# Block 0 of a fused attention and GLU kernel loaded as pairs of tokens, with attention by token parity and the gate by tanh

## The chip, the cores and the metric

The kernel runs on one core of one Trainium2 chip. The metric is the device time of one execution, in microseconds (us), as the median of several executions. The kernel before repeats within 0.4%.

Engines: PE is TensorE's matmuls, PEld its weight loads, DVE VectorE, ACT ScalarE, POOL GpSimd, SP SyncE. POOL, SP and ACT also issue the DMA loads and stores.

## The reference

Linear attention with decay over four batches, eight heads, 768 tokens and head size 64, then a gated feed-forward layer over the 3072 tokens (512 to 1536 to 512):

```python
# attention, per batch and head, token i, j <= i:
out[i] = sum_j (q[i] . k[j]) * lam[h] ** (i - j) * v[j]      # computed in blocks, with a state
x      = out.transpose(0, 2, 1, 3).reshape(B * S, H * D)
# feed-forward
gate = 1.0 / (1.0 + np.exp(-(x @ w_gate)))
val  = x @ w_val
return (gate * val @ w_out).astype(np.float32)
```

## The kernel before

Tokens are taken in six blocks of 128 per batch. Block 0's attention comes first, alone; then, for each block, twelve slices of gate and value products, four output products, and the next block's attention woven in between. The opening is what the argument touches: the loads of q, k and v of block 0, one token per partition, so 64 numbers, 256 bytes, per piece.

```python
def load(n, what, b0=0, b1=B):
    ...
        if b0 < nat:
            nc.gpsimd.dma_start(out=T_[c, n][:, b0:nat],
                in_=src[b0:nat, :, sl, :].rearrange("b h s d -> s (b h) d"))
...
load_hw("k", 0, nc.sync)          # k of batch 0, fp32, issued by SyncE
nc.scalar.dma_start(out=lam_bc, in_=lam.partition_broadcast(128))
load_hw("k", 1, nc.scalar)        # k of batch 1, issued by ScalarE
load(0, "q", 0, 2)                # the rest by GpSimd, cast to bf16 on the way
... identity, iotas, selects ...
load(0, "k", 2, 4)
load(0, "q", 2, 3); load(0, "q", 3, 4)
load(0, "v", 0, 2); load(0, "v", 2, 3); load(0, "v", 3, 4)
for ft in range(4):
    load_gv(ft, ft + 1)           # weights of the first slices: WG, WV
```

While these loads are on their way, PE is kept going with products of zeros (`zeros(9)` first). The gate of a slice and the loads of a later block:

```python
nc.scalar.activation(sg, gp, AF.Sigmoid)                 # sg in bf16
nc.vector.tensor_mul(HT[n, ft], sg, vp)
...
def next_loads(n):                # called for n = 2 in the slices of block 1
    xbar(n)                       # DMA transposes of q and k
    gate(n)                       # POOL waits here for the transposes
    load(n, "v")
    if n + 1 < NSTEP:
        load(n + 1, "qk")
```

## Time and profile before

| | before |
|---|---|
| time | 224.5 us median (224.48 to 224.63) |
| span in the profile | 222.8 us |
| first gate product starts | 15.23 us |
| gate products of blocks 1, 2, 3 start | 52.65, 86.69, 120.67 us |
| last output product ends | 219.86 us |

The rows below the first two are read from the timeline of PE, by the names of the tiles (gp for gate). From block to block PE needs 34 us.

### The profile page before, as it was taken

The page shows a single profiled execution, that of the slowest core. Times are in us where ns is not written, and L with a number is a line of the kernel's source. Part 1 is how long each engine was busy: PE and PEld are TensorE (multiplying, and loading weights), DVE is VectorE, ACT ScalarE, POOL GpSimd, SP SyncE. Part 2 cuts the span into 40 slices and gives each one's busy share as a digit, 9 for nine tenths or more (in the row PEclk, how much of TensorE's full clock was granted, in tenths as well). Part 3 has the DMA queues.
Part 4 walks back from the last instruction along what each step waited for, and adds up shares of the span by engine and source line. Part 5 has one row for each costly group of instructions (what it writes and reads, how often), then busy time and mean ns, then how long its engine had stood idle before and what let it go on. Part 6 is the DMA issues. An engine that isn't in the chain of part 4 may idle for free.

```text
span 222.8 us, 5208 instructions
## 1 busy us (share of the span) xinstructions
PE 215.8 (97%) x2187; PEld 105.7 (47%) x2187; DVE 104.4 (47%) x196; ACT 106.4 (48%) x232; POOL 64.0 (29%) x83
## 2 busy tenths in 40 slices
PE   6799999999999999999999999999999999999994
PEld 1454444557444544444544444544444544444443
DVE  4885652539777600785700686700676400333301
ACT  5877434594384523385433376342366342333221
POOL 7999855660094006700940030000000000000000
PEclk9999999999999999999999999999999999999999
DMA  6999999999989997999899995012100012100022
GB/s 108 152 169 182 195 203 178 175 156 156 176 55 158 235 153 214 179 162 176 56 157 231 223 63 36 3 50 94 47 3 0 3 50 94 47 0 0 4 94 96
DMA packets 106008, 25.25 MB, mean 113 GB/s; under 512 B 97152, under 2 KB 103552, under 8 KB 105984
## 3 DMA queue, kind: packets, MB, share of 16 engines
q0 software_dynamic: 82944, 13.90, 81.1%
q1 hardware_dynamic: 21712, 10.69, 20.4%
q10 hardware_dynamic: 1328, 0.33, 0.7%
q8 instruction: 17, 0.28, 0.5%
q14 instruction: 7, 0.06, 0.1%
HBM read 28.32 MB, written 6.29 MB: 155 GB/s over the span
## 4 chain that ended last, share of the span: by engine, by line
PE 91%; POOL 4%; DMA 3%; issue 1%; ACT 0%; POOLq 0%
PE po L523 28%; PE vp L488 28%; PE gp L488 28%; DMA WV<-in_moe_w_val_dram 3%; POOL vb L96 1%; PE sp L387 1%; PE cp L447 1%; PE op L411 1%; PE op L425 1%; POOL qb L96 1%; POOL WG L107 1%; POOL kb L96 1%; PE cp L363 1%; PE sp L310 0%; PE op L341 0%
## 5 line engine op out<-in xcount | busy, mean ns | idle before, releaser
L488 PE MATMUL gp<-XT,WG 128*128 128x512 bf16 (+1 forms) x296 | 74.2, 374 | 0.3 <-ACT XT L588 0.3
L488 PE MATMUL vp<-XT,WV 128*128 128x512 bf16 (+1 forms) x292 | 74.1, 376 | 0.1
L500 ACT ACTIVATE sg<-gp 128x512 bf16<-128x512 f32 x72 | 43.0, 597 | 62.9 <-PE gp L488 62.9
L505 DVE TENSOR_TENSOR ht<-sg,vp 128x512 bf16<-128x512 bf16 x48 | 33.0, 687 | 79.9 <-PE vp L488 76.9
L523 PE MATMUL po<-WO,ht 128*128 128x512 bf16 (+2 forms) x300 | 63.9, 371 | 0.0
L488 PEld LDWEIGHTS <-WV 128*128 128x128 bf16 x292 | 28.5, 98 | 33.7 <-DMA WV<-in_moe_w_val_dram 0.6
L523 PEld LDWEIGHTS <-ht 128*128 128x128 bf16 x300 | 28.3, 98 | 31.9
L488 PEld LDWEIGHTS <-WG 128*128 128x128 bf16 x296 | 28.2, 98 | 31.9 <-DMA WG<-in_moe_w_gate_dram 0.7
L527 ACT COPY ob<-po 128x512 f32<-128x512 f32 (+1 forms) x24 | 13.7, 572 | 38.8 <-PE po L523 38.8
L129 ACT ACTIVATE kd<-kb,kds 128x128 bf16<-128x128 bf16 (+1 forms) x88 | 28.9, 401 | 0.0
L503 DVE TENSOR_TENSOR ht<-sg,vp 128x512 bf16<-128x512 bf16 x24 | 16.5, 687 | 13.5 <-PE vp L488 13.3
L616 POOL COPY gates<-qt 128x1 bf16<-128x1 bf16 x4 | 0.8, 188 | 49.0 <-DMA qt<-qb 49.0
L96 POOL DMA_DIRECT2D vb<-in_v_dram x9 | 11.9, 1334 | 2.8 <-issue 1.7
L318 DVE TENSOR_TENSOR MT<-sp,mask 128x512 bf16<-128x512 f32 x16 | 9.9, 684 | 3.0 <-PE sp L310 3.0
L437 ACT CAST XT<-op 128x512 bf16<-128x512 f32 x16 | 8.2, 599 | 5.0 <-PE op L425 5.0
L397 DVE TENSOR_TENSOR MT<-sp,mask 128x512 bf16<-128x512 f32 x16 | 10.3, 683 | 0.0
L102 POOL DMA_DIRECT2D qb<-in_q_dram x10 | 8.8, 892 | 3.4 <-DMA WO<-in_moe_w_out_dram 3.2
L96 POOL DMA_DIRECT2D qb<-in_q_dram x8 | 8.9, 1115 | 1.8 <-POOLq L757 0.8
L102 POOL DMA_DIRECT2D kb<-in_k_dram x10 | 8.9, 913 | 1.1 <-DMA WG<-in_moe_w_gate_dram 0.6
L537 PE MATMUL zps<-st 128*128 128x512 bf16 x18 | 6.1, 471 | 1.5 <-DVE st L161 1.5
L96 POOL DMA_DIRECT2D kb<-in_k_dram x6 | 7.0, 1174 | 0.5 <-DMA WG<-in_moe_w_gate_dram 0.5
L110 POOL DMA_DIRECT2D WV<-in_moe_w_val_dram x9 | 7.1, 807 | 0.2 <-issue 0.2
(81 smaller groups left out, 114.3 us busy)
## 6 DMA issues: line engine op xcount, KB each, us to landing
out_dram<-ob SPq DMA_DIRECT2D x19, 256.0 KB, 2.3
vb<-in_v_dram POOLq DMA_DIRECT2D x4, 512.0 KB, 7.4
qb<-in_q_dram POOLq DMA_DIRECT2D x6, 256.0 KB, 7.7
kb<-in_k_dram POOLq DMA_DIRECT2D x6, 256.0 KB, 9.2
qb<-in_q_dram POOLq DMA_DIRECT2D x12, 128.0 KB, 7.5
WO<-in_moe_w_out_dram POOLq DMA_DIRECT2D x4, 384.0 KB, 12.3
kb<-in_k_dram POOLq DMA_DIRECT2D x10, 128.0 KB, 9.4
WG<-in_moe_w_gate_dram POOLq DMA_DIRECT2D x4, 256.0 KB, 7.0
```

What stands on the lines that cost most here:

```text
L96: nc.gpsimd.dma_start(out=T_[c, n][:, b0:nat], in_=src[b0:nat, :, sl, :].rearrange("b h s d -> s (b h) d"))
L102: nc.gpsimd.dma_start(out=T_[c, n][:, m:b1, u::2, :], in_=src[m:b1, 1 - u::2, sl, :].rearrange("b h s d -> s (b h) d"))
L129: nc.scalar.mul(KD[n][:, at, i, :], T_["k", n][:, at, i, :], kds[:, min(n // FIRST_XBAR, 1), h:h + 1])
L318: nc.vector.tensor_tensor(out=MT[n, b][:, u], in0=SP[n, b][u], in1=mask0[:, 1 - u if swapped(n, b) else u], op=ALU.mult)
L397: nc.vector.tensor_tensor(out=MT[n, bp][:, u], in0=SP[n, bp][u], in1=mask[:, u ^ bp].unsqueeze(1).to_broadcast([128, 2, HP, L]), op=ALU.mult)
L437: nc.scalar.copy(XT[n][:, c, :, bp * C:(bp + 1) * C], OP[n, c, bp].rearrange("p h j i -> p h (j i)"))
L488: nc.tensor.matmul(ps[:, part], lhsT=W[:, mt, fs], rhs=XT[n][:, part, mt], start=(part is not second and mt == 0), stop=(part is not first ...
L500: nc.scalar.activation(sg, gp.rearrange("p a b -> p (a b)"), AF.Sigmoid)
L503: mul = nc.vector.tensor_mul(HT[n, ft], sg, vp.rearrange("p a b -> p (a b)"))
L505: mul = nc.vector.tensor_mul(HT[n, ft].rearrange("p (b c i) -> p c b i", b=B, c=2), sg.rearrange("p (c b i) -> p c b i", c=2, b=B), vp.rea ...
L523: nc.tensor.matmul(po[:, :c1 - c0], lhsT=HT[n, ft][:, tt * 128:(tt + 1) * 128], rhs=WO[:, ft, c0:c1], start=(ft == 0), stop=(ft == NFT - 1))
L527: (eng.copy if eng is nc.scalar else eng.tensor_copy)(o, po[:, :c1 - c0])
```

## The change

Its intent: block 0's loads read two neighbouring tokens per partition, so 512 bytes per piece instead of 256, since DMA looks like what holds the opening. Partition p holds tokens 2p and 2p+1; partitions 0 to 63 hold the even heads, 64 to 127 the odd ones. The attention of block 0 is then done in 64x64 tiles by token parity. Most tables move behind the first slices. The gate becomes (tanh(x/2) + 1) / 2, with tanh in the same table set as exp.

```diff
+    def pairs(src, b0, b1):
+        return src[b0:b1, :, 0:C, :].rearrange("b (r g) (p e) d -> g p b r (e d)", g=2, e=2)
+    def load0(c, b0, b1):
+        ...
+        for g in range(2):                       # two halves of 64 partitions
+            nc.gpsimd.dma_start(out=T_[c, 0][rows_of(g), b0:b1]...,
+                                in_=src[g].rearrange("p b r x -> p (b r) x"))
     def load_hw(c, b, eng):
-        eng.dma_start(out=H32[c, b], in_=src[b, :, 0:C, :].rearrange("h s d -> s h d"))
+        for g in range(2):
+            eng.dma_start(out=H32[c, b][rows_of(g)]..., in_=pairs(src, b, b + 1)[g, :, 0])
...
+    nc.scalar.preload_act_table_set("exp_and_others")      # early
-    nc.scalar.preload_act_table_set("sigmoid_and_others")  # was in the masks
...
-                nc.scalar.activation(sg, gp..., AF.Sigmoid)
+                nc.scalar.activation(sg, gp..., AF.Tanh, scale=0.5)      # sg now fp32
-            mul = nc.vector.tensor_mul(HT[n, ft], sg, vp...)
+        mul = gate_value(HT[n, ft], sg, vp...)  # scalar_tensor_tensor: (sg + 1) * vp
-            (eng.copy ...)(o, po[:, :c1 - c0])
+            (eng.mul ...)(o, po[:, :c1 - c0], 0.5)
...
-    zeros(9)
+    zeros(6)
... t_0, s_0, a_0, c_0: block 0's transposes, scores, outputs and state in 64x64 tiles
... store_0: block 0's rows stored by parity, 14 stores instead of 8
```

The two halves per load follow from the layout: heads go with the half, so a single load for both halves has a source with one stride more.

## The prediction

> **What bounds the kernel now.** I read the page first, then the chain that ended last, then the waits and the timeline of the first 18 us. Columns of the page's first part: busy us, share, instructions.
>
> ```profile
> span 222.8 us, 5208 instructions
> PE 215.8 (97%) x2187; PEld 105.7 (47%) x2187; DVE 104.4 (47%) x196; ACT 106.4 (48%) x232; POOL 64.0 (29%) x83
> ```
>
> PE is full: 97% with no other engine over half. The chain in order of time (start, us, what) shows where PE is not yet the limit:
>
> ```profile
> 7.14 2.90 POOL vb L96 x3
> 10.04 0.75 POOL WG L107
> 10.79 0.74 POOL WV L110
> 11.53 0.67 POOL WG L107
> 12.21 5.81 DMA WV<-in_moe_w_val_dram
> 18.02 0.05 issue
> 18.07 1.04 PE vp L488 x4
> 19.10 0.86 PE gp L488 x4
> ```
>
> Up to 18.07 the chain runs over POOL, which issues the loads, and one weight transfer; from there it is matmuls, 0.86 us for each group of four, to the end. So **a change can only win by starting the first gate product (15.23 us) earlier, by removing holes just behind it, or by removing PE work.** The waits between 14 and 30 us (total us, times, longest) name the holes:
>
> ```profile
> PEld L488 <- DMA WG<-in_moe_w_gate_dram: 0.7, 2, 0.5
> PEld L488 <- DMA WV<-in_moe_w_val_dram: 0.6, 1, 0.6
> PEld L585 <- DMA vb<-in_v_dram: 0.4, 1, 0.4
> PE gp L488 <- ACT XT L588: 0.3, 1, 0.3
> ```
>
> Everything just before the first product waits for loads: the last v, the first WG, and the second WV (PE should have gone on at 17.85 and starts at 18.07: 0.2 us lost). The same loads seen from DMA, in the stretch 8 to 13 us:
>
> ```profile
> DMA packets 6137, 0.78 MB, mean 155 GB/s; under 512 B 6137, under 2 KB 6137, under 8 KB 6137
> q0 software_dynamic: 6137, 0.78, 243.5%
> ```
>
> That is 1227 pieces per us, 128 bytes written each (256 read). The stretch 14 to 17 us, which carries weights (512 bytes read, 256 written), has 707 pieces per us and 180 GB/s. In both DMA is busy in every slice, and the issues land 5 to 6 us after they are made: **a backlog, so DMA and not POOL sets the landings today**, though the chain, which follows issue by issue, prints POOL.
>
> [...] The gate product takes 687 ns for 512 elements, while 1024 elements of bf16 from SBUF take 685 ns (the scaling of QS)[...], and the gate in fp32 rather than bf16 should cost nothing there.
>
> **The change part by part.**
>
> *Pieces.* After the change a batch (256 KB read) is 512 pieces instead of 1024. At the rates above it takes 0.72 us of DMA (512/707) instead of 0.83 (1024/1227). The 10 batches of q, k and v that POOL loads cost 7.2 us instead of 8.3. DMA gains 1.1 us, and something on the two k batches that SP and ACT load.
>
> *Issues.* A half of the partitions per issue makes 14 issues out of 7. POOL's start-to-start times before: 0.735 us for a weight slice of 512 pieces (10.00, 10.74, 11.47, 12.21), 0.93 for 1024 (two in 1.87), 1.15 for 2048. So about 0.60 plus 0.27 per 1024 pieces, a fit of mine. Then 512 pieces cost 0.74, 256 cost 0.67. New: 6 halves of two batches, 4.4; 8 halves of one batch, 5.4; sum 9.8 us. Old: 1.28 + 1.15 + 1.87 + 2.87 = 7.2. Plus 2.6. POOL's own operations ahead of the first weight (identity, three iotas, two selects: 8.75 less 7.2, some 1.6 us) shrink to identity and one iota, some 0.6. Net: the first WG is issued at 1.25 + 9.8 + 0.6 = 11.65 us, not at 10.00.
>
> *Landings.* POOL now feeds a single batch in 1.34 us (two halves) that DMA moves in 0.72, so the backlog disappears and a landing is its issue plus an unloaded lag. The v load at 128.69, alone on the queue, gives that lag: issue ends at 130.38, the first packets come after 131.0, the last about 135.1, it lands at 135.8. So 0.8 ahead of the transfer and 0.7 behind it, plus up to 0.3 of ramp. First WG: 11.65 + 0.74 + 0.8 + 0.72 + 0.7, ramp included about 14.9 (before: 10.00 + 5.2 = 15.2). Last v: issued by 11.65, lands about 13.7 (before 14.4). Second WV: 11.65 + 3 x 0.74, lands about 17.1, needed at gp start + 2.6 = 17.5: the 0.2 us hole goes. Gates 4 and 5: issued after eight slices (5.9) and the iotas moved here (0.8), at 18.35, plus 0.74 + 0.8 + 1.44 + 0.7, 22.0; needed 7 groups and the split one later, gp start + 6.9 = 21.8. A hole of 0 to 0.4 us can open there.
>
> *The attention of block 0.* DVE: eight mask products of 0.68 each. Before they ran 8.85 to 11.33 and 11.89 to 14.37, the second stretch held by the q loads. Now q lands earlier (2: about 9, before 10.3), so both stretches run nearly as one, from about 8.5 to 13.8; two evictions behind them give about 14.8. ACT gains a second table load (1.28 us, at about 4.6, before exp) and loses the one at 12.32, and 4 of 5 early exps of 0.32 each move behind the products. DVE gets four wide exponents instead of eight narrow ones of 344 ns. PE's tiled products double in number at half the size: chunks of other blocks do 64 products of 64x64 in 0.74 us, so 16 take about 0.3 with latency, as before. The swap product (0.39) was in a hole anyway. None sets the end alone, but all meet near 14.8 to 15.0.
>
> *Steady state.* tanh for sigmoid, fp32 gate, factor 0.5 in the eviction: same element counts; 0.60 on ACT and 0.69 (perhaps 0.75) on DVE against 1.73 us of PE per slice. Eight query tables come behind slices 6 and 7, 1.28 us each plus 0.60 is 1.88, over 1.73 by 0.15, absorbed by a spare PSUM buffer. The state update K=64 has 64 products in about 0.7 us against 0.63 before. Stores go from 8 to 14 on SP, 0.66 us each: the transposes behind come 4 us later; the earlier (q) lands at about 88 and is used at 92.74. Hidden.
>
> *Sum.* First product 15.23 to about 14.95: minus 0.3. Hole at 17.85: minus 0.2. Hole at gates 4: plus 0.1 on average. 224.5 - 0.3 - 0.2 + 0.1 = **224.1 us**.
>
> **Rivals.** (1) *DMA alone counts*: if issues in halves are cheaper than my fit, or DMA was the only limit, v and WG land 1 us or more earlier. DVE then bounds: 5.5 us of products and two evictions. 223.0 to 223.4. For it: saturated DMA today. Against: the 0.735 us issue hardly falls with pieces. (2) *POOL takes DMA's place and is worse*: if a half costs 0.85 instead of 0.7, the first WG lands 2 us later than reckoned, and so does gates 4: 225.5 to 226. For it: slice issues did drift from 0.79 to 0.87 while the queue was full. Against: it will not be full. (3) *Row tiles collide*: two 64-row tiles write one PSUM bank in the output and state products. [...] The old chunk code gives each row tile its own bank, so this trace cannot tell. Serial, 16 products take about 0.9 instead of 0.4: plus 0.5 on the last batch, plus 2 on the state update; 225 to 226.5. (4) *Nothing*: all cancels, 224.4.
>
> **Range and chances.** PE after 15.23 is untouched, so 2% (4.5 us) faster would need the first product before 11 us, when not even the masks are done. Slower by 4.5 needs rivals 2 and 3 together and a new hole. The range spans from rival 1 to mild 2 or 3: **222.9 to 225.4**. Faster 0.02, within 2% 0.95, slower 0.03.
>
> **What would show it.** Right: POOL's L-lines of block 0 with 14 halves of about 0.7 us each; first WG issued near 11.65 and landing within 3.5 us of its issue, not 5.2; DMA below full between 6 and 13 us; first gate product at 14.6 to 15.2; no wait for the second WV; PE busy unchanged to 1 us. Wrong: landings still 5 us behind issues (the backlog stayed), a gate product before 14.2, a wait for gates 4 over 0.5 us, output products in the start over 0.8 us per batch, or PE waiting for DVE or ACT after 20 us.

The 1.28 us of a table load are those of the two in the trace before, at 1.68 and 12.32 us.

## More of the kernel before

The prediction shows the page, the chain and the waits. Here is the opening's timeline before, cut to the key and query path (kb, tk: keys; qb, tq: queries; zps: products of zeros; MT: the first of the products with the masks). Columns: start, duration, engine (SPq is SyncE issuing), line, operation, out<-in, count; in brackets the engine's idle time before it and what ended that.

```profile
0.74 0.45 SPq L152 DMA_DIRECT2D h<-in_k_dram  x1
1.53 3.49 PE L537 MATMUL zps<-st 128*128 128x512 bf16 x9 [1.53 <-DVE st L161]
5.37 0.41 DVE L293 CAST kb<-h 128x512 bf16<-128x512 f32 x1
5.84 0.40 PE L267 MATMUL tk<-ident,kb 128*128 128x128 bf16 x4 [0.82 <-DVE kb L293]
...
7.45 0.62 PE L267 MATMUL tq<-ident,qb 128*128 128x128 bf16 x8 [0.56 <-DMA qb<-in_q_dram]
...
8.85 2.48 DVE L318 TENSOR_TENSOR MT<-sp,mask 128x512 bf16<-128x512 f32 x4 [0.54 <-PE sp L310]
...
15.23 1.05 PE L488 MATMUL gp<-XT,WG 128*128 128x256 bf16 x8 [0.30 <-ACT XT L588]
```

The first queries (tq at 7.45) are waited for; from there everything to the first gate product follows in 7.78 us. PE is idle for only 0.82 us after the first zeros.

The load stream in the stretch 11 to 18 us, before:

```profile
DMA packets 6341, 1.19 MB, mean 170 GB/s; under 512 B 6340, under 2 KB 6340, under 8 KB 6340
```

## The result, and the profile after

The kernel after gives correct results and takes **228.11 us** (227.43 to 228.66, four runs) against 224.56 us (224.48 to 224.69, four runs) in the same rounds: ratio 1.0156, 95% interval 1.0127 to 1.0185. A ratio is the mean time of one kernel's runs over that of the other's of the same rounds, so it is not quite the ratio of the medians quoted. Executions over 1.5% slower than the fastest of the same kernel are left out of the means. That is still within the 2% band, but 3.5 us slower, outside the range of 222.9 to 225.4. It also spreads over 1.2 us, the kernel before over 0.2.

| | before | after |
|---|---|---|
| span in the profile | 222.8 | 225.7 |
| first gate product | 15.23 | 17.48 |
| gate products of block 1 | 52.65 | 54.74 |
| of block 2 | 86.69 | 89.51 |
| of block 3 | 120.67 | 123.49 |
| last output product ends | 219.86 | 222.68 |

So 2.25 us are lost before the first gate product, 0.16 come back in block 0, 0.73 are lost in block 1, and nothing from block 2 on. (The profiled execution, 227.43 us, was the fastest of the four.)

The page's first part after:

```profile
span 225.7 us, 5469 instructions
PE 216.6 (96%) x2302; PEld 107.3 (48%) x2311; DVE 104.4 (46%) x192; ACT 107.8 (48%) x236; POOL 65.7 (29%) x89
```

PE's busy time has grown by 0.8 us only: the rest is idle time of PE. The opening's timeline after, the same path:

```profile
0.74 1.45 SPq L167 DMA_DIRECT2D h<-in_k_dram  x2
1.25 1.50 POOL L114 DMA_DIRECT2D qb<-in_q_dram  x2 [0.81 <-POOLq L812]
1.53 2.74 PE L608 MATMUL zps<-st 128*128 128x512 bf16 x6 [1.53 <-DVE st L177]
6.80 0.70 DVE L363 CAST kb<-h 128x512 bf16<-128x512 f32 x1 [2.58 <-DMA h<-in_k_dram]
7.56 0.64 PE L290 MATMUL tk<-ident,kb 128*64 128x128 bf16 x8 [3.28 <-DVE kb L363]
8.13 1.46 PE L608 MATMUL zps<-st 128*128 128x512 bf16 x3
...
8.46 3.22 POOL L114 DMA_DIRECT2D vb<-in_v_dram  x5 [0.52 <-DMA qb<-in_q_dram]
...
9.52 1.06 PE L290 MATMUL tq<-ident,qb 128*64 128x128 bf16 x16
...
11.69 5.05 DVE L307 TENSOR_TENSOR MT<-sp,mask 128x512 bf16<-128x512 f32 x8 [1.06 <-PE sp L300]
...
17.48 1.12 PE L558 MATMUL gp<-XT,WG 128*128 128x256 bf16 x8
```

Three things differ. SyncE takes 1.45 us to issue the keys of batch 0 in two halves (before 0.45 in one), and the cast waits for them until 6.80 (before it could run at 5.37). PE is idle for 3.28 us. And then PE is slow: three products of zeros take 1.46 us, where three took 0.81 before. They start 0.43 us apart here, 0.22 in the steady state (0.86 us for each group of four). I call the first half rate and the second full rate; a warm PE is one that runs at full rate. The kernel before starts at half rate too: its first zeros are 0.43 us apart up to 4.43 us, after 2.9 us of zeros (in a_warm below it takes 5.4). The six zeros of the kernel after end before that, at 4.27, and none of them is faster. So this trace does not show PE at full rate before the gap at all; whether it fell in the gap or had never risen stays open. The page's row of the granted clock does not help in these two kernels; it reads 9 (90% or more) in every slice of both, over the slow first zeros as well. So that the missing zeros and the idle gap made PE slow is a reading, which a_warm below tests.

The issues on POOL: the load of q starts at 1.25, as before, and takes 1.50 us in two halves (before 1.28 in one). Between two halves of v, POOL stands 0.52 us until the queries have landed, at 8.17 us; why it has to wait for them, the runs leave open. The first WG is issued at 11.65 us. The load stream in the stretch 8 to 13 us, and in 11 to 18 us:

```profile
DMA packets 3183, 0.78 MB, mean 155 GB/s; under 512 B 3183, under 2 KB 3183, under 8 KB 3183
q0 software_dynamic: 3183, 0.78, 160.8%
...
DMA packets 3561, 0.89 MB, mean 127 GB/s; under 512 B 3560, under 2 KB 3560, under 8 KB 3560
```

In the first stretch half the pieces carry the same bytes. In the second, DMA moves 0.89 MB where it moved 1.19 before. The row of its busy share still reads 9 in most slices, but the time of its packets falls from 204.2% of the engines' span to 136.6%. I read this as DMA not being fed; a_best2 below supports it.

The waits between 14 and 30 us hold no load at all any more; the first of PE's are of 0.2 to 0.4 us behind work of ACT and its own issue. PE starts so late that all weights are there. But the chain of work that ended last has changed. In order of time, before 72 us:

```profile
2.06 6.11 DMA qb<-in_q_dram
...
20.38 6.25 DMA WG<-in_moe_w_gate_dram
...
30.88 13.49 DMA WO<-in_moe_w_out_dram
...
45.52 9.94 DMA qb<-in_q_dram
...
58.86 4.92 DMA kt<-kb
...
64.19 7.14 DMA vb<-in_v_dram
71.33 0.04 issue
71.37 0.73 PE cp L514 x60
```

Before, the chain went over to PE at 18.07. After, it runs along the loads until 71.33, where the values of block 2 land, and the state products that need them (cp) start at once. In the kernel before these values land at about 69.1 (issued at 62.01, 7.1 us to landing), and cp starts at 69.12. Counted from the start of the last group ahead of it that is 1.01 us; the same change from 128x128 to 64x64 products takes 0.95 to 0.96 where nothing is waited for (62.16 to 63.12, 74.11 to 75.06). So cp waited 0.05 us at most for them. In b_tanh, which takes the same time, PE waits 0.22 us for them, at 69.33. **So the kernel before stood at two limits at once**, PE and the load stream, and its chain printed PE's side of a near tie. In the trace after, both came late together.

A last 0.3 us: the first products of the attention of block 2 have a hole of 0.32 us at 78.24 which waits for nothing in the profile. Of the other kernels' profiles only a_kwide's has it (0.82 us at 79.59). I did not find its cause.

### The profile page after: what moved, and what is told of

Same layout as the page of the kernel before. It is cut to its first block, busy times and chain, and to the rows that moved or that the text cites. A ratio compares the mean times of both kernels' runs of the same rounds, so it can differ in the third digit from the quotient of the medians.

```text
span 225.7 us, 5469 instructions
## 1 busy us (share of the span) xinstructions
PE 216.6 (96%) x2302; PEld 107.3 (48%) x2311; DVE 104.4 (46%) x192; ACT 107.8 (48%) x236; POOL 65.7 (29%) x89
## 4 chain that ended last, share of the span: by engine, by line
PE 67%; DMA 21%; POOL 7%; issue 2%; SPq 1%; ACT 0%; POOLq 0%
PE po L594 23%; PE gp L558 20%; PE vp L558 20%; DMA qb<-in_q_dram 7%; DMA WO<-in_moe_w_out_dram 6%; DMA vb<-in_v_dram 3%; DMA WG<-in_moe_w_gate_dram 3%; DMA kt<-kb 2%; POOL WV L121 2%; POOL WG L118 2%; SPq L368 1%; POOL vb L114 1%; PE op L478 1%; PE cp L514 1%; PE op L492 1%
## 5 line engine op out<-in xcount | busy, mean ns | idle before, releaser
L548 DVE SCALAR_TENSOR_TENSOR ht<-sg,vp 128x512 bf16<-128x512 f32 x72 | 49.4, 686 | 92.9 <-PE vp L558 90.0
L570 ACT ACTIVATE sg<-gp 128x512 f32<-128x512 f32 x72 | 43.0, 597 | 59.5 <-PE gp L558 59.5
L598 ACT ACTIVATE ob<-po 128x512 f32<-128x512 f32 (+1 forms) x24 | 14.0, 583 | 38.7 <-PE po L594 38.7
L143 ACT ACTIVATE kd<-kb,kds 128x128 bf16<-128x128 bf16 x80 | 25.2, 390 | 0.0
L464 DVE TENSOR_TENSOR MT<-sp,mask 128x512 bf16<-128x512 f32 x16 | 10.3, 682 | 0.0
L96 POOL DMA_DIRECT2D vb<-in_v_dram x6 | 9.0, 1501 | 3.3 <-issue 1.6
L102 POOL DMA_DIRECT2D qb<-in_q_dram x10 | 8.8, 893 | 2.9 <-DMA WO<-in_moe_w_out_dram 2.9
L102 POOL DMA_DIRECT2D kb<-in_k_dram x10 | 8.9, 913 | 1.2 <-DMA WG<-in_moe_w_gate_dram 0.6
L539 DVE SCALAR_TENSOR_TENSOR st<-st,pow_l,cp 128x128 bf16<-128x128 bf16 x24 | 6.7, 341 | 0.0
L118 POOL DMA_DIRECT2D WG<-in_moe_w_gate_dram x8 | 6.6, 825 | 0.0
L96 POOL DMA_DIRECT2D kb<-in_k_dram x5 | 5.9, 1180 | 1.5 <-issue 1.2
L96 POOL DMA_DIRECT2D qb<-in_q_dram x5 | 5.8, 1153 | 0.4 <-DMA WO<-in_moe_w_out_dram 0.4
```

Source lines behind the costliest of these rows:

```text
L96: nc.gpsimd.dma_start(out=T_[c, n][:, b0:nat], in_=src[b0:nat, :, sl, :].rearrange("b h s d -> s (b h) d"))
L102: nc.gpsimd.dma_start(out=T_[c, n][:, m:b1, u::2, :], in_=src[m:b1, 1 - u::2, sl, :].rearrange("b h s d -> s (b h) d"))
L118: nc.gpsimd.dma_start(out=WG[:, :, f0 * 128:f1 * 128], in_=wg_r[:, :, f0 * 128:f1 * 128])
L143: nc.scalar.mul(KD[n][:, at, i, :], T_["k", n][:, at, i, :], kds[:, min(n // FIRST_XBAR, 1), h:h + 1])
L464: nc.vector.tensor_tensor(out=MT[n, bp][:, u], in0=SP[n, bp][u], in1=mask[:, u ^ bp].unsqueeze(1).to_broadcast([128, 2, HP, L]), op=ALU.mult)
L548: return nc.vector.scalar_tensor_tensor(out=o, in0=g, scalar=1.0, in1=x, op0=ALU.add, op1=ALU.mult)
```

## The experiments

Fourteen kernels ran. Names that begin with b_ start from the kernel before, those with a_ from the kernel after. "Wide" means one load over all 128 partitions. Wide loads of pairs bring the wrong tokens (0 to 255 of the even heads), the same bytes in the same pieces to the same places, so those kernels give wrong results; they tell what the halves cost.

### b_rows: the halves alone, in the kernel before

```diff
-                nc.gpsimd.dma_start(out=T_[c, n][:, b0:nat], in_=src[b0:nat, :, sl, :]...)
+                for g in range(2):   # block 0 only, tokens 0..63 and 64..127; k by SP and ACT too
+                    nc.gpsimd.dma_start(out=T_[c, n][rows_of(g), b0:nat],
+                                        in_=src[b0:nat, :, g * 64:(g + 1) * 64, :]...)
```

> The kernel before with only this taken from the change: every block 0 load (two k batches on the hardware queues, q, k and v on POOL) is issued as two halves of 64 partitions each; pieces stay 256 bytes, layout and result stay right. Theory A (halves are slow[...]): the first k batch lands at 6.0 us or later instead of 4.84, DMA in 5 to 12 us falls below 155 GB/s, first gate product 1.5 to 3 us later, total 226 to 227.5. Theory B (only the second issue and its queueing cost): the same as with the split by heads or batches, b_heads. Theory C (the delay of the change comes from its 512-byte pieces, its tiled products or its order of work): first k batch within 0.5 us of 4.84 and total within 1 us of 224.5.

Measured: correct, 227.82 us (227.76 to 228.22); before 224.72; ratio 1.0140 (1.0120 to 1.0159). The first WG is issued at 13.01 us (before 10.00), and PE waits for WG before and after the first gate product (0.86, 0.62 and 0.28 us). The halves alone cost about as much as the whole change, a little more than theory A expected. The path is another one, though: the first query transposes start at 7.93 us, only 0.48 later than before, and the first gate product comes 9.15 us after them (before 7.78), because its weights come last.

### b_heads: as many issues, but over all partitions

```diff
+                    one = nat - b0 == 1
+                    bb = slice(b0, nat) if one else slice(b0 + g, b0 + g + 1)
+                    hs = slice(4 * g, 4 * g + 4) if one else slice(0, H)
+                    nc.gpsimd.dma_start(out=T_[c, n][:, bb, hs], in_=src[bb, hs, sl, :]...)
```

> The kernel before with as many issues as b_rows and the same 256-byte pieces, but each half over all 128 partitions: loads of two batches are cut into single batches, loads of one batch and the hardware k loads into heads 0-3 and 4-7. Result right. Theory A (partition halves): first k batch within 0.5 us of 4.84, DMA stays at 150 to 156 GB/s, total at most 225.5, clearly under b_rows by 1 us or more. Theory B (number of issues): the same as b_rows within 0.5 us, first k batch near 6 us or later.

Measured: correct, 229.70 us (228.97 to 230.19); ratio 1.0217 (1.0190 to 1.0244). That is what neither theory expected. The same number of issues split another way is slower still: here an issue takes 0.94 us for q, where a half of the partitions took 0.87, and the first WG goes out at 14.11. So for POOL's loads it is not the half of the partitions that costs, but the issues. For the two k loads on SP and ACT it is the other way round: two full-width loads take 0.50 us each to issue and the first cast runs at 5.41; two halves take 0.70 each and the cast runs at 6.57.

### b_tanh: the gate alone, in the kernel before

The edit is the gate, output and table-set lines of the diff above, with the table load at its old place, and the order of columns in `chunk_x` that goes with it.

> The kernel before with only the gate of the change: tanh of half the gate product, fp32 gate, (gate + 1) times value, factor 0.5 in the output eviction, the chunk order of the activations that this form needs, and the second table load naming the exp set at its old place. Result right. My theory: off the path, 224.5 within 0.5 us, gate product on DVE 0.69 us as before. Rival: the larger gate or the strided eviction costs PE waits, over 225.5.

Measured: correct, 224.74 us (224.67 to 224.78); ratio 0.9998 (0.9977 to 1.0019). The gate product's row of the groups (count, busy us, mean ns), first b_tanh, then the kernel after:

```profile
L481 DVE SCALAR_TENSOR_TENSOR ht<-sg,vp 128x512 bf16<-128x512 f32 x72 | 49.5, 687 | 93.3 <-PE vp L491 90.3
```
```profile
L548 DVE SCALAR_TENSOR_TENSOR ht<-sg,vp 128x512 bf16<-128x512 f32 x72 | 49.4, 686 | 92.9 <-PE vp L558 90.0
```

It was 687 ns with a bf16 gate too. The gate part costs nothing and gains nothing.

### a_warm: the kernel after with more zeros

```diff
-    zeros(6)
+    zeros(17)
```

> The changed kernel with 17 instead of 6 zero products ahead of the first transposes, so that PE has no idle stretch before the first k batch (6 products end at 4.27, PE then sat idle for 3.28 us, and its later products of 512 columns started 0.43 us apart, not 0.22). Result right. Theory D (the idle stretch leaves PE at half speed through the opening, which delays the tiled products and the fillers between them): fillers at 8 to 9.5 us start 0.22 us apart, the mask products on DVE start near 10.9 instead of 11.69, first gate product 16.6 to 17.0 instead of 17.48, total 227.0 to 227.6. Rival (late loads alone count): first gate product within 0.2 us of 17.48, total as the change, 228.1.

Measured: correct, 227.55 us (226.60 to 228.57); ratio 1.0122 (1.0087 to 1.0158). Its opening:

```profile
7.91 0.41 PE L290 MATMUL tk<-ident,kb 128*64 128x128 bf16 x8
8.26 0.82 PE L608 MATMUL zps<-st 128*128 128x512 bf16 x3
9.01 0.64 PE L290 MATMUL tq<-ident,qb 128*64 128x128 bf16 x16
```

PE runs at full rate (0.82 us for three products of zeros, not 1.46), and the first gate product comes at 16.83 instead of 17.48. Both are as expected. PE does not wait for the queries here: they land at 8.52 us, and the zeros hold PE until 9.01. The time falls by only 0.56 us in the medians, and the intervals of the two ratios overlap, so a gain in time is not shown. In the profiled run (the slowest of the four) PE waits 1.01 us for WG at 24.95 and 0.98 us for the values of block 2, which land at 72.79. So the late loads are a limit of their own.

### a_wide and a_wide_warm: the kernel after with wide loads

```diff
         src = {"q": q, "k": k, "v": v}[c]
-        for g in range(2): ...
+        nc.gpsimd.dma_start(out=T_[c, 0][:, b0:b1].rearrange("p b (r e) d -> p (b r) (e d)", e=2),
+                            in_=src[b0:b1, 0::2, 0:2 * C, :].rearrange("b r (p e) d -> p (b r) (e d)", e=2))
         # the k loads on SP and ACT likewise; a_wide_warm also: zeros(6) -> zeros(9)
```

> The changed kernel with every block 0 load as one issue over 128 partitions with 512-byte pieces: it reads tokens 0 to 255 of every second head, so its result is wrong on purpose; bytes, pieces and the work behind are those of the change. Theory A or B (halves or issues are what costs): first k batch lands by 5 us, first gate product at 14 to 15.2 us instead of 17.48, total 222.5 to 224.5. Theory C (order of work, clock or tiled products): first gate product after 16.5 us, total over 226.5.

> As a_wide (all block 0 loads full width, wrong result on purpose), with 9 zero products instead of 6. Theory D: mask products on DVE start near 9 us and run nearly as one stretch, first gate product at 14 to 15 instead of 17.78, total 223.2 to 224.4, below the kernel before: 512-byte pieces would then be a gain if a full-width load could bring them. Rival (a_wide was slow for another reason, say the tiled products or one more table load): first gate product after 16.5, total over 225.5.

Measured: a_wide 225.94 us (225.12 to 227.42), ratio 1.0060 (1.0016 to 1.0103); a_wide_warm 224.93 us (224.77 to 225.08), ratio 1.0005 (0.9990 to 1.0020). Both wrong (relative error 0.41). The load stream of a_wide_warm in the stretch 11 to 18 us:

```profile
DMA packets 4966, 1.25 MB, mean 179 GB/s; under 512 B 4946, under 2 KB 4965, under 8 KB 4965
```

The times miss the ranges expected, a_wide_warm's by 0.5 us. With seven issues DMA is fed and moves 1.25 MB, against 0.89 with fourteen and 1.19 before. In a_wide's profiled execution PE was at half rate for most of 8 to 14 us, although no idle gap after its first products was over 1.6 us, against 3.28 in the kernel after (from 5 to 8 us it was busy for 1.16 of 3 us); why, the runs leave open. Here the row of the granted clock shows it (6 and 7 tenths in two slices; 0.50 from 8.0 to 14.0 us), and here PE had been at full rate before: three products of zeros at 6.14 take 0.82 us. In a_wide_warm, three products of zeros more, PE was not at half rate from there on (three products of zeros take 0.82 us at 6.08 and at 11.54), and the first gate product comes at 14.87 instead of 17.78. That is where the change was meant to bring it. The times of a_wide spread over 2.3 us, those of a_wide_warm over 0.3. From four executions each I take it that the zeros keep the rate up, though I can't exclude that a_wide's profile, the slowest of its four runs, caught a slow opening by chance: its first queries land at 8.06 us, and those of a_wide_warm are used at 7.19, with the very same loads. So one profile places such a landing only to within 0.9 us. Still a_wide_warm's time is that of the kernel before, not 0.36 us less:

```profile
69.14 0.73 PE L512 MATMUL cp<-vb,kd 64*64 64x64 bf16 x64 [0.52 <-DMA vb<-in_v_dram]
```

PE waits 0.52 us for the values of block 2. They land at 69.1, as in the kernel before, and hand the gain back: issued 0.65 us sooner (61.36), they take 7.7 us instead of 7.1, for a reason that the runs leave open. **Wide loads and a warm PE take away the whole loss**; tiles, tables, gate and stores cost nothing that shows.

### a_kwide and a_kwide_warm: only the k loads on SP and ACT wide

```diff
         H32[c, b] = hwp.tile([128, H, D], FP32, tag="h32", name="h32")
-        for g in range(2): ...
+        eng.dma_start(out=H32[c, b].rearrange("p (r e) d -> p r (e d)", e=2),
+                      in_=src[b, 0::2, 0:2 * C, :].rearrange("r (p e) d -> p r (e d)", e=2))
         # a_kwide_warm also: zeros(6) -> zeros(9)
```

> The changed kernel with only the two hardware k loads as one issue each over 128 partitions (wrong tokens, wrong result on purpose); POOL loads stay in halves, zeros stay at 6. Theory A for the k loads alone: first k batch lands by 5 us instead of 6.7, and with it the cast. If late k is all that holds the opening, the first gate product comes 1.5 us or more earlier, at 15.5 to 16. Theory D says less: PE is still slow, as in a_wide (first product 17.78 in spite of early loads), so 16.5 to 17.8.

> As a_kwide, with 9 zero products as before the change instead of 6 (wrong result on purpose). If late k and the half speed of PE together are the loss: first gate product at 15.0 to 15.6, total 224.3 to 225.2. If the halves of the POOL loads or the tiled products cost on their own: still after 16.3, total over 226.

Measured: 228.68 us (228.41 to 229.14), ratio 1.0173 (1.0151 to 1.0194), and 228.18 us (227.76 to 228.53), ratio 1.0149 (1.0129 to 1.0168). The keys of batch 0 are cast at 5.80 and 5.64 us, a microsecond sooner than in the kernel after, and the time is no better. In both PE was at half rate in the opening all the same (until 9.5 us in a_kwide, from 8.4 to 14 in a_kwide_warm; the sixteen query transposes take 1.06 us in both, 0.64 in a_warm), so these two do not separate the clock from the keys. In a_kwide's profile the first gate product comes at 16.60 us, 0.88 sooner than in the kernel after and within what theory D said; it is lost again by block 2, with a wait of 0.56 us for the same values of block 2 and the hole of 0.82 us told above. So earlier keys alone gain at the first product and nothing in the time. In a_kwide_warm it comes at 18.21, so the first of its two expectations (15.0 to 15.6) failed. Nine products of zeros did not keep this opening warm.

### a_few: fewer issues, correct

```diff
-    load0("q", 2, 3); load0("q", 3, 4)
-    load0("v", 0, 2); load0("v", 2, 3); load0("v", 3, 4)
+    load0("q", 2, 4)
+    load0("v", 0, 2); load0("v", 2, 4)
-    zeros(6)
+    zeros(17)
```

> The kernel after with the queries of batches 2 and 3 in one load instead of two, and the values of batches 2 and 3 too: 10 issues on GpSimd for block 0 instead of 14, the same bytes, the same 512-byte pieces, the same two halves of 64 partitions; and 17 opening zero products, as in a_warm, so that TensorE stays at full rate. Correct results. Theory (what costs is the number of issues on GpSimd, which cannot feed the queue, and the loss is paid at the load of the values of block 2, which the whole stream of loads ends in): the four issues of 0.61 to 0.69 us that go let the first WG load be issued at about 9.1 instead of 11.65 us; the stream is some 1.5 us further on at 18 us; the values of block 2 land at 70 to 71.3 instead of 72.8, and the time is 225.5 to 226.4 us against 227.6 of a_warm. Rival (the halves themselves are slow to land, however few issues there are): within 0.4 us of a_warm.

Measured: correct, 226.28 us by the median of four, but one of these, the profiled one, took 580.67 us, with every product of 512 columns near 0.6 us; the three fast runs are 225.98, 226.14 and 226.41, ratio 1.0071 (1.0055 to 1.0086). I draw nothing from the slow execution. The median of the fast runs, 226.14 us, is 1.4 us below a_warm's, in the expected range, and the intervals of the two ratios just do not overlap: four issues fewer, some 1.4 us gained, the same halves and pieces.

### a_best: and the halves of a key load on two engines at once

```diff
+    load_hw("k", 0, nc.sync, 0);  load_hw("k", 0, nc.scalar, 1)      # one half each
     nc.scalar.dma_start(out=lam_bc, in_=lam.partition_broadcast(128))
+    load_hw("k", 1, nc.sync, 0);  load_hw("k", 1, nc.scalar, 1)
     # as a_few, with zeros(13)
```

> a_few, with the two halves of each key load of batches 0 and 1 issued side by side, one by SyncE and one by ScalarE, instead of one behind the other on one engine; 13 opening zero products. Correct results. Theory: the keys of batch 0 land at 5.2 to 5.8 instead of 6.7 us, [...]the first gate product comes at 15 to 15.8 us; the time then hangs on the load of the values of block 2 alone, as in a_few: 225.3 to 226.2 us. Rival (the halves take as long to land side by side[...]): keys at 6.5 us or later and no better than a_few.

Measured: correct, 226.56 us (226.20 to 227.07), ratio 1.0089 (1.0076 to 1.0103), above the range expected. The keys come early (cast at 4.56 us), PE stays at full rate (three products of zeros at 7.26 take 0.82 us), and the load of the values of block 2 is no longer waited for. But I had put the load of lam behind a key load on ACT's queue, and the logarithms of lam wait for it:

```profile
6.78 0.42 ACT L206 ACTIVATE lns<-lam_bc 64x4 f32<-64x4 f32 x2 [2.69 <-DMA lam_bc<-in_lam_dram]
```

The masks come late, PE waits 0.39 and 0.90 us ahead of the scores, and the first gate product is at 17.09. The cast of the keys was not the path; a fault of the experiment took its place.

### a_wide_split and b_split: the values of block 2 in two loads

```diff
         gate(n)
-        load(n, "v")
+        if n == 2:
+            load(n, "v", 0, 2); load(n, "v", 2, 4)
+        else:
+            load(n, "v")
```

a_wide_split is a_wide_warm with this edit, b_split the kernel before with it.

> a_wide_warm (224.93 us; wrong results on purpose, as there) with the load of the values of block 2 issued as two loads of two batches, so that the half that the first state products of block 2 read lands about 3.5 us sooner. Nothing else changes. Theory (that landing is the second bound; the wait of 0.52 us ahead of those products is what gave the earlier start back): the wait goes, the gate products of block 2 start at 86.3 instead of 86.8, and the time is 224.3 to 224.6 us. Rival (another bound stands right behind, or the earlier start was lost elsewhere): 224.8 to 225.1 us.

> The kernel before with only that split of the load of the values of block 2. Correct results. In the kernel before the products that wait for this load start at 69.12, 0.14 us after the products ahead of them can have ended, so at most 0.15 us is to be had: 224.3 to 224.6 us, no difference that the rounds can show. Said by both theories of the kernel after; it tells how close to its own second bound the kernel before ran. A version that beats it would have to be earlier at both bounds.

Measured: a_wide_split 224.42 us (224.28 to 225.09; wrong), ratio 0.9998 (0.9985 to 1.0010); b_split correct, 224.71 us (224.49 to 224.92), ratio 1.0005 (0.9991 to 1.0019), beside 224.64 for the kernel before. In a_wide_split the median is 0.5 us below a_wide_warm's, inside the expected range; four of its five runs lie at 224.28 to 224.60. The fifth, which the profile shows, lost 0.39 us ahead of its first gate product, waiting for WG, so the expected 86.3 us for block 2 was missed (87.07). Its state products start at 68.94 without a wait, but the second of the two loads lands only at 69.43, and its chain still runs over it:

```profile
63.12 6.31 DMA vb<-in_v_dram
...
69.47 0.45 PE cp L512 x32
```

So in this profile the split shortened the wait and did not end it. The interval of the ratio includes no change: nothing is shown to be faster than the kernel before. In the kernel before the edit does nothing, as expected: there PE is not ahead of the load.

### a_wide_q: which load sets the first gate product

```diff
+        if c == "q" and b0 == 0:       # a_wide_warm with this one load in two halves
+            for g in range(2): nc.gpsimd.dma_start(... rows_of(g) ...)
+            return
```

> a_wide_warm (224.93 us, wrong results on purpose, as there) with one load alone put back as two halves of 64 partitions: the queries of batches 0 and 1, the first on GpSimd. Theory (the landing of these queries sets the first gate product in a warm opening): they land at 8.3 to 8.9 us instead of 7.2, the first gate product comes 7.7 us after, at 16.0 to 16.6 instead of 14.87; the loads behind are about 0.5 us later too, so the values of block 2 still cost some wait; the time is 225.6 to 226.4 us. Rival (the sum of all issues on GpSimd counts, one load makes little): first gate product at 15.4 us or before, time below 225.4 us.

Measured: 225.94 us (225.67 to 226.73; wrong), ratio 1.0060 (1.0040 to 1.0080). The first query transposes start at 8.56 instead of 7.19 us, the first gate product at 16.05 instead of 14.87, and the wait for the values of block 2 is 0.19 us. All as expected: one load in two issues costs 1.0 us of time. But POOL is held by that load for 0.48 us longer only (1.49 instead of 1.01); the rest of the 1.37 us lies between issue and landing, where one profile is uncertain by up to 0.9 us (a_wide), and no run separates it.

### a_best2: the nearest correct version

```diff
     # a_best with lam first, the split of a_wide_split, zeros(11)
+    nc.scalar.dma_start(out=lam_bc, in_=lam.partition_broadcast(128))
     load_hw("k", 0, nc.sync, 0);  load_hw("k", 0, nc.scalar, 1)
-    nc.scalar.dma_start(out=lam_bc, in_=lam.partition_broadcast(128))
```

> a_best with the load of lam ahead of the half of a key load on ScalarE (in a_best it landed at 6.76 us, and the exponents and masks waited for it), 11 opening zero products instead of 13, and the load of the values of block 2 in two halves of two batches as in a_wide_split. Correct results. Theory (the landing of the queries is what is left): lam lands at 3.8 us, keys of batch 0 at 4.8 to 5.5, queries at 8.3 to 8.8, first gate product at 16.0 to 16.6, no wait for the values of block 2, time 225.4 to 226.0 us: still behind the kernel before. Rival (a_best lost its time to the late lam and the load of block 2 alone): first gate product at 15.3 us or before and 224.3 to 224.8 us, as fast as the kernel before.

Measured: correct, 225.31 us (225.08 to 225.35), before 224.73 in the same rounds; ratio 1.0024 (1.0010 to 1.0037). Just under the range expected.

```profile
5.15 0.56 DVE L364 CAST kb<-h 128x512 bf16<-128x512 f32 x1 [0.93 <-DMA h<-in_k_dram]
7.98 0.64 PE L291 MATMUL tq<-ident,qb 128*64 128x128 bf16 x16 [1.04 <-DMA qb<-in_q_dram]
...
15.96 1.12 PE L559 MATMUL gp<-XT,WG 128*128 128x256 bf16 x8
```

The queries are still half a microsecond behind those of the kernel before (7.98 against 7.45), as they come in two issues (in a_wide_q that alone made it 8.56 for 7.19). The kernel after was 3.55 us behind the kernel before of its rounds, this one is 0.58 behind: ten issues instead of fourteen, the keys side by side and a warm PE have taken back 3.0 of it. In the stretch 11 to 18 us it moves 1.25 MB, as much as a_wide_warm with its seven issues, and so does a_best. While the loads of block 0 themselves are moving, from 6 to 8 us, the halves of a_best2, a_warm and the kernel after come at 173 to 176 GB/s, the full-width loads of a_wide and a_wide_warm at 164 and 181. So the halves are not moved more slowly; what is left of theory A is the issues. No version of the change tried here beats the kernel before.

## Why the prediction was wrong, point by point

**The issues: right.** Fourteen halves, 0.60 plus 0.27 us per 1024 pieces: the first WG goes out at 11.65 us, the very number predicted. That it fits to the digit is luck: the issues took 9.2 us instead of the 9.8 reckoned, and POOL stood 0.52 us for the queries, which the sum did not have. The halves, of 256 and 512 pieces, took 0.61 to 0.81 us each; a load of 2048 in the kernel before took 1.28. Rival 2, a half at 0.85, did not come; and yet POOL did take DMA's place.

**The landings: right for v, short for the weights.** The backlog did shrink: four of the halves of v land 3.1 us after their issue. The first WG lands 4.0 us after its issue, at 15.65, where 14.9 and at most 3.5 us were named, and the weights behind it 4.9 (median). DMA's busy share did not fall below full between 6 and 13 us either.

**The start of the mask products: the step that failed first.** "Now q lands earlier (2: about 9, before 10.3), so both stretches run nearly as one, from about 8.5 to 13.8; two evictions behind them give about 14.8." The eight mask products on DVE did run as one, in 5.05 us, but from 11.69 to 16.74; in the kernel before they start at 8.85. So the first gate product came at 17.48 us and not at 14.95. The sum reckoned landings for the last loads, v and WG. Nothing in it stood for the first keys and the first queries, in halves now, or for PE's work on them. In the kernel after the queries land at 8.17, but PE, held by late keys and at half rate, takes them at 9.52. In these five kernels with a warm PE the first gate product follows the first query transposes by about the same time:

| | tq starts | gp starts | between |
|---|---|---|---|
| before | 7.45 | 15.23 | 7.78 |
| a_wide_warm | 7.19 | 14.87 | 7.68 |
| a_wide_q | 8.56 | 16.05 | 7.49 |
| a_warm | 9.01 | 16.83 | 7.82 |
| a_best2 | 7.98 | 15.96 | 7.98 |

In four of them PE waits for the queries to land, in a_warm the zeros hold it; in b_rows the weights come last, as told there. a_wide_q shows it with one load alone: 1.37 us later queries, 1.18 us later gate product. The prediction gave minus 0.3 us for this product, and with wide loads and a warm PE it is minus 0.36. With the halves it is plus 1.6 (a_warm), and plus 2.25 with the slow PE.

**The keys on SP and ACT: a term left out.** "DMA gains 1.1 us, and something on the two k batches that SP and ACT load." They lost: 1.45 us of issue instead of 0.45, and a cast that starts at 6.80 instead of 5.37 us.

**PE's clock: a term left out.** The diff cuts the opening products of zeros from nine to six. I did not ask what they are for. With late keys, PE stood idle for 3.28 us and ran at half rate after it, as it had before it. More zeros brought the first gate product 0.65 us forward (a_warm). In time they gained 0.56 us in the kernel after and 1.01 with wide loads (a_wide_warm), by the medians; neither is clear of the spread. a_kwide_warm went slow with nine products of zeros too, and the slow openings may be why the kernel after spreads over 1.2 us; that part I have only argued.

**"From there it is matmuls ... to the end", and "PE after 15.23 is untouched": false.** The chain of the kernel before showed one side of a near tie. The load stream runs without slack to the values of block 2. When POOL could not feed it (0.30 MB less in 11 to 18 us), these values came 2.2 us later in the trace after, and 3.7 later in a_warm's, with PE waiting. 0.30 MB at the 196 GB/s of the stretch 24 to 26 us is about 1.5 us, so that lag can explain most of the 2.2. It works against gains too: a_wide_warm was 0.36 us ahead at its first product and had lost that by 69.14.

**The 0.2 us hole at the second WV: gone, for another reason.** PE now comes so late that the weights are there. The same holds for gates 4 and 5.

**The rest: right.** tanh, the fp32 gate and the output factor are neutral (b_tanh). The tiles do not collide (rival 3): 64 output products of block 0 take 1.98 us, about 0.5 per batch and not 0.9. They are of 128 columns, so one after another they would take some 3.5 us, an estimate from the 0.216 us of 512 columns (0.86 for four): the two row tiles overlap, though for three of the four batches they write the two halves of one PSUM tile. PE's busy time is within 1 us. The chances were right as far as they went: the result is within 2%. The range was not, since both its ends were reckoned from PE's side of the tie, with a warm PE, and for the loads that came last only.

## What to carry to other kernels

Where loads have to be issued in twice as many instructions, count the issuing engine's time (9.2 us here for fourteen issues, 7.2 for seven) for the first load that is waited for as well as the last, and see that the queue stays fed afterwards (0.89 MB in 11 to 18 us, before 1.19). A chain of waits shows one path: where a transfer lands within a few tenths of the product that needs it (0.05 us here), there is a second path as long, and gains ahead of it are handed back (the 0.36 us of a_wide_warm). Filler products at the start went with the rate of TensorE here: the three products of zeros behind the first keys took 1.46 us in the kernel after, which starts with six, and 0.82 in a_warm, which starts with seventeen; in a_kwide_warm nine did not keep it at full rate (half rate from 8.4 us). So they belong to the timing of the loads they bridge, and when a load moves, they must move with it.
